# Factor blocks split into gates and the rest, with y outputs copied earlier and the maximum of h taken earlier, in a fused attention and two-MoE kernel

## The chip, the cores and the metric

The kernel runs on one core of a Trainium2 chip. Its engines each work through a queue of their own in order: TensorE (PE) multiplies matrices, VectorE (DVE), ScalarE (ACT) and GpSimd (POOL) do elementwise work, and SyncE (SP) issues most DMA transfers; ACT issues those of y. The metric is the device time of one execution in microseconds (us), less is better.

## The reference

Three stages follow one another over 4608 tokens, all in float32. Weights of the two MoE stages come as float64.

```python
# attention in chunks of 64 tokens, 8 heads of 64
scores = scale * np.matmul(q_c, k_c.transpose(0, 1, 2, 4, 3))
attn = softmax(scores);  x = attn @ v_c          # x: 4608 x 512
# first MoE
h = x @ w_in                                     # 4608 x 1024
e = np.exp(h - h.max(-1));  solu = h * e / e.sum(-1)
ln = (solu - mu) / np.sqrt(var + 1e-06) * g_ln
y = ln @ w_out                                   # 4608 x 512
# second MoE
g = y @ w_gate;  val = y @ w_val                 # 4608 x 1536
out = (g * sigmoid(g) * val) @ w_out2            # 4608 x 512
```

## The kernel before

Every product is made of three passes over a high part and a low part of each operand, so each weight and each result has to be split: ACT copies the high part, then DVE or POOL subtracts it from the value to leave the low part.

**Phase 1** makes y, 128 tokens at a time, in 36 slots, `slot(t)` for t = 0 to 35. From slot 3 on the engines' queues follow the order in which the code is written (`manual_schedule`). In one slot TensorE does, in order:

- `scores(t+2)`: s, for a tile of tokens two slots ahead
- `hidden(t)`: h, 24 matmuls
- `ln_T(t-1)`: tr, eight transposes of the slot before
- `pv(t+1)`: o, attention times v
- `y_run`: 32 of y's matmuls. An output y takes 24 of them, so it ends in the middle of a slot; the matmuls already done of the current output at the start of a slot are 0, 8 or 16, in turn. This number is called the slot's **y phase**: it is 0 in slots 10, 13, 16 and so on to 34, 8 in slots 11, 14, ..., and 16 in slots 12, 15, ...
- `p_transpose(t+2)`: pt, four transposes of the softmax. pt shares two PSUM buffers (tag `y`) with the outputs y, and takes the one of the output that ended first in this slot, so it needs the copy of that output (ACT, `ysb`, L162).

Around these, DVE takes the maximum and the difference of s (mx, e), converts one weight (L103, L109, L114, L120), sums the softmax (su, r), takes the maximum of h (nm, L341), finishes the layer norm's first half (se to nmu, so), and makes low parts (lnT, x). ACT does exp of e, exp of h (eh), copies lnT and x, squares (eh, L369, called the Square below), takes the sign off the next weights (L87), copies ysb and pbd. POOL adds the halves of a converted weight (L130, L133), scales e (L284; pt needs it) and finishes the layer norm (L371 to L383).

From slot 8 on each slot also converts one or two pieces of the second MoE's weights, 36 in all: for each of twelve factors f a **gate** piece g, a **value** piece v and an **out** piece o. `w2_out` gives g and v their places in one tile `blk` of eight parts (tag `blk`, one buffer): two for the gate (a11, a12), two for the value (a21, a22) and four for sums (s1 to s4), the operands of a Strassen-like product with seven products instead of eight. In the slot after the value's, three steps follow (`w2_spill`): `sums` makes s1 to s4 on DVE (L208), `high` copies seven parts on ACT into `shi` (L211) and stores them, `low` subtracts on DVE (L215) and stores them; both stores go to `ws_dram`. That slot is called a **spill slot** here. The pieces of seven slots, after which the pattern comes again with the next three factors:

| slot | 10 | 11 | 12 | 13 | 14 | 15 | 16 |
| --- | --- | --- | --- | --- | --- | --- | --- |
| converted | o0 | g1, v1 | o1 | g2 | v2, o2 | g3 | v3 |
| sums, high, low of | f = 0 | | f = 1 | | | f = 2 | |

So 17 is like 10, 18 like 11 and so on; the spill slots from 10 to 33 are 10, 12, 15, 17, 19, 22, 24, 26, 29, 31 and 33. The first piece of a slot is added on POOL ahead of the scaling of e, a second one at the slot's end.

In slots 0 to 5 the same three steps serve the first MoE's w_out (`split_scaled`): step 0 scales on ACT (L137), step 1 splits into wB on ACT and POOL (L71, L73), which `y_run` multiplies by from slot 5 on.

**Phase 2** reads y and the factors back and does the second MoE in six groups of tokens, `step(s, f)` for twelve f each, seven products per step from tiles `wsa` (the first four parts) and `wsb` (the other three).

Of the kernel before, what the change touches and what calls it, by code (L numbers as in the profile page):

```python
# [8 lines left out]
F32 = mybir.dt.float32  # L9
F32R = mybir.dt.float32r  # L10
# [3 lines left out]
AF = mybir.ActivationFunctionType  # L14
ALU = mybir.AluOpType
AX = mybir.AxisListType

P = 128
# [8 lines left out]
def attn_moe_moe2_kernel(  # L27
# [13 lines left out]
    nc = tc.nc  # L41
# [103 lines left out]
    NY = 3 * KF  # L145
# [22 lines left out]
    KH = KD // 2 * P  # L168
    NS = 7
    ws_dram = [dram.tile([P, NS, 2, KH], F32, tag=f"ws{f}", name=f"ws{f}") for f in range(FT)]  # L170
# [3 lines left out]
        f, j = divmod(u, 3)  # L174
        return raw_load(stage, (w_gate, w_val, w_out2)[j][f])

    blks = {}

    def w2_out(u):

        f, j = divmod(u, 3)
        if j == 2:
            return None
        if f not in blks:
            blks[f] = stage.tile([P, NS + 1, KH], F32, tag="blk", name="blk", bufs=1)
        return blks[f][:, 1:6:4] if j == 0 else blks[f][:, 0:8:7]

    def w2_spill(u, w):

        f, j = divmod(u, 3)  # L190
        if j == 0:
            return None
        if j == 2:
            hi = stage.tile([P, DM], F32R, tag="m", name="wohi", bufs=4)
            src, dst = w, wo_dram[f]
        else:
            b = blks.pop(f)
            hi = stage.tile([P, NS, KH], F32R, tag="shi", name="shi", bufs=1)
            src, dst = b[:, 1:], ws_dram[f].rearrange("p s b n -> p b s n")

        def sums():
            if j == 1:
                a21, a11, s1, s2, s3, a12, s4, a22 = (b[:, i] for i in range(NS + 1))
                for o, x, y, op in (
                    (s1, a21, a22, ALU.add), (s3, a11, a21, ALU.subtract),
                    (s2, s1, a11, ALU.subtract), (s4, a12, s2, ALU.subtract),
                ):
                    nc.vector.tensor_tensor(out=o, in0=x, in1=y, op=op)  # L208

        def high():  # L210
            nc.scalar.activation(out=hi, in_=src, func=AF.Copy)  # L211
            nc.sync.dma_start(out=dst[:, 0], in_=hi.bitcast(F32))

        def low():
            nc.vector.tensor_tensor(  # L215
                out=src.bitcast(F32R), in0=src, in1=hi.bitcast(F32), op=ALU.subtract
            )
            nc.sync.dma_start(out=dst[:, 1], in_=src)

        return sums, high, low  # L220

    with ExitStack() as ph1:
# [97 lines left out]
        def hidden(t, halves=(0, 1)):  # L320
            x = xt[t]
            if 0 in halves:
                ht[t] = ps_h.tile([P, DF], F32, tag="h", name="h")
            h = ht[t]
            for n in halves:
                i = 0
                for k in range(KD):
                    for a, b in PASSES:
                        nc.tensor.matmul(  # L329
                            h[:, n * DM:(n + 1) * DM], lhsT=x[:, a, k, :],  # L330
                            rhs=wA[:, n * KD + k, b, :],
                            start=(i == 0), stop=(i == 3 * KD - 1),
                        )
                        i += 1
            if 1 in halves:
                del xt[t]

        def ln_max(t):
            h = ht[t]
            nm = sm.tile([P, 1], F32, tag="nm", name="nm")  # L340
            nc.vector.tensor_reduce(out=nm, in_=h, axis=AX.X, op=ALU.max, negate=True)  # L341
            st["nm", t] = nm

        def ln_exp(t):
            h, nm = ht[t], st.pop(("nm", t))
            e = hp_.tile([P, DF], F32, tag="eh", name="eh", bufs=1)
            se = sm.tile([P, 1], F32, tag="se", name="se")
            nc.scalar.activation(out=e, in_=h, func=AF.Exp, bias=nm, accum_out=se)  # L348
            st["e", t] = e, se
# [93 lines left out]
        def y_upto(t):  # L443

            return max(0, min((NG - 1) * KD * NY, (t - GT) * KD * NY // GT)) if t >= W_OUT else 0
# [65 lines left out]
        wB = wblock(lastp, "B", KF)  # L511
# [14 lines left out]
        def slot(t, todo2):  # L526


            todo, ahead = w_todo(t), t + 2 < NT
            cs = conv.pop(t)  # L530
            outs = [w2_out(u) if k == "2" else None for k, u in todo]
            if ahead:
                scores(t + 2)
                if t + 4 < NT:
                    load_qk(t + 4)
                softmax(t + 2)
            cs[:1] = [conv_c(c, o) for c, o in zip(conv_b(cs[:1]), outs)]
            if ahead:
                softmax_b(t + 2)
            if t > 0:  # L540
                hidden(t)
            for k, steps in todo2:
                steps[0]()
            ln_max(t)
            ln_exp(t)
            ln_low = ln_T(t - 1) if t >= 1 else None
            ln_b(t)
            x_low = None
            if t + 1 < NT:
                pv(t + 1)  # L550
                if t + 3 < NT:
                    load_v(t + 3)
                x_low = x_split(t + 1)
            if ln_low:
                ln_low()
            if x_low:
                x_low()
            ln_c(t)
            for k, steps in todo2:
                steps[1]()  # L560
            if t + 1 < NT:
                conv_start(t + 1)
            cs[1:] = [conv_c(c, o) for c, o in zip(conv_b(cs[1:]), outs[1:])]
            y_run(wB, y_upto(t - 1), y_upto(t), ps_y, att)
            for k, steps in todo2:
                steps[2]()
            if t + 2 < NT:
                raws[t + 2] = w_raw(t + 2)
                p_transpose(t + 2)
            todo2 = []  # L570
            for (k, u), w in zip(todo, cs):
                if k == "o":
                    a, b = split_scaled(wB[:, u], w, g_sb[:, u:u + 1])
                    todo2.append((k, (a, b, lambda: None)))
                elif steps := w2_spill(u, w):
                    todo2.append((k, steps))
            return todo2
# [14 lines left out]
    with ExitStack() as ph2:  # L592
# [22 lines left out]
        def w_load(s, f):  # L615
            if f >= FT:
                s, f = s + 1, f - FT
            if s >= NSG:
                return
            if s == 0:  # L620
                nc.sync.dma_start(out=wout(f).bitcast(F32), in_=wo_dram[f])
            a = cp.tile([P, 4, 2, KH], F32R, tag="wsa", name="wsa", bufs=3)
            b = cp.tile([P, 3, 2, KH], F32R, tag="wsb", name="wsb", bufs=3)
            nc.sync.dma_start(out=a.bitcast(F32), in_=ws_dram[f][:, 0:4])
            nc.sync.dma_start(out=b.bitcast(F32), in_=ws_dram[f][:, 4:7])
            ws[s, f] = [a[:, i] for i in range(4)] + [b[:, i] for i in range(3)]

        def y_load(s):
            for kk in range(2):
# [196 lines left out]
```

## Time and profile before

| | |
| --- | --- |
| Median of three runs | 1539.91 us (1539.21 to 1540.45) |
| The profiled execution: its own time | 1538.05 us |
| The profiled execution: its span | 1536.1 us |
| Busy share of the span | PE 91%, DVE 59%, ACT 36%, POOL 32% |
| Mean granted TensorE clock | 0.957 of full speed |

The span is what the trace covers; 1.95 us of the profiled execution lie around it. A timeline row has the start and the duration in us, the engine, the line, out<-in, the shapes, the count, and in brackets the idle time ahead and what ended it. A row of windows has the stretch and its length, the busy us (and count) of PE, PEld (weight loads), DVE, ACT and POOL, the granted clock as a share of full speed, the DMA share and GB/s.

Slots are told apart in the trace by the start of their score matmuls: slot 10 starts at 205.84 us, slot 34 at 653.15 (it has no scores, so there its first matmul of h counts), phase 2's first product at 707.24.

### The profile page before, as it was taken

The page shows a single profiled execution, that of the slowest core. Times are in us where ns is not written, and L with a number is a line of the kernel's source. Part 1 is how long each engine was busy: PE and PEld are TensorE (multiplying, and loading weights), DVE is VectorE, ACT ScalarE, POOL GpSimd, SP SyncE. Part 2 cuts the span into 40 slices and gives each one's busy share as a digit, 9 for nine tenths or more (in the row PEclk, how much of TensorE's full clock was granted, in tenths as well). Part 3 has the DMA queues.
Part 4 walks back from the last instruction along what each step waited for, and adds up shares of the span by engine and source line. Part 5 has one row for each costly group of instructions (what it writes and reads, how often), then busy time and mean ns, then how long its engine had stood idle before and what let it go on. Part 6 is the DMA issues. An engine that isn't in the chain of part 4 may idle for free.

```text
span 1536.1 us, 21457 instructions
## 1 busy us (share of the span) xinstructions
PE 1403.2 (91%) x7920; PEld 1268.5 (83%) x7920; DVE 903.4 (59%) x1620; ACT 560.2 (36%) x1116; POOL 484.4 (32%) x597
## 2 busy tenths in 40 slices
PE   3578998979869878899999999999999999999998
PEld 2457877858758767789998999899999989999997
DVE  8863577757656765755446444644644464455442
ACT  4443444524525443444223232322322242333221
POOL 5553334334333424433113122321411132232211
PEclk9788999979989998999999999999999999999999
DMA  7311345345544443349773556456455635554531
GB/s 243 115 41 45 110 137 178 105 153 153 168 125 153 155 144 114 109 159 401 249 253 132 203 176 215 154 174 221 148 185 192 232 126 202 176 205 165 173 136 42
DMA packets 122936, 252.02 MB, mean 164 GB/s; under 512 B 45520, under 2 KB 79312, under 8 KB 113616
## 3 DMA queue, kind: packets, MB, share of 16 engines
q1 hardware_dynamic: 115920, 241.21, 47.2%
q10 hardware_dynamic: 6912, 9.44, 1.7%
q8 instruction: 63, 1.03, 0.3%
q14 instruction: 41, 0.34, 0.1%
HBM read 203.43 MB, written 47.19 MB: 163 GB/s over the span
## 4 chain that ended last, share of the span: by engine, by line
PE 63%; DVE 7%; issue 3%; ACT 3%; DMA 2%; POOL 2%; SPq 0%; ACTq 0%; DVEq 0%; POOLq 0%
PE o L723 13%; PE pa L657 10%; PE pd L657 10%; PE pc L657 10%; PE tail L723 6%; PE h L329 5%; PE pb L657 5%; PE y L156 2%; DVE so L359 1%; PE s L260 1%; ACT eh L348 1%; DVE blk L208 1%; DVE nm L341 1%; ACT shi L211 1%; DMA ws<-blk 1%
## 5 line engine op out<-in xcount | busy, mean ns | idle before, releaser
L329 PE MATMUL h<-wA,x 128*128 128x512 f32 x864 | 229.4, 424 | 25.3 <-DVE wA L473 12.7
L329 PEld LDWEIGHTS h<-wA,x 128*128 128x128 f32 x864 | 173.5, 205 | 73.3 <-DVE wA L473 13.8
L156 PE MATMUL y<-lnT,wB 128*128 128x384 f32 x1152 | 212.3, 341 | 7.6 <-POOL wB L73 3.6
L156 PEld LDWEIGHTS y<-lnT,wB 128*128 128x128 f32 x1152 | 201.0, 190 | 14.1 <-issue 5.1
L714 POOL TENSOR_TENSOR uflow<-sa,uflow 128x384 fp32r<-128x384 f32 x72 | 73.5, 1021 | 414.0 <-ACT uflow L685 392.8
L714 DVE TENSOR_TENSOR uflow<-sb,uflow 128x128 fp32r<-128x128 f32 x72 | 28.2, 391 | 228.8 <-ACT uflow L712 228.8
L693 POOL TENSOR_TENSOR u<-u,p 128x384 f32<-128x384 f32 x72 | 73.0, 1014 | 192.2 <-DVE u L692 183.6
L723 PE MATMUL o<-wo,uflow 128*128 128x512 f32 x504 | 122.8, 392 | 0.0
L682 ACT ACTIVATE p<-pa 128x384 f32<-128x384 f32 x72 | 35.5, 492 | 233.1 <-PE pa L657 231.1
L348 ACT ACTIVATE eh<-h,nm 128x1024 f32<-128x1024 f32 x36 | 40.2, 1116 | 195.6 <-DVE nm L341 195.6
L723 PEld LDWEIGHTS o<-wo,uflow 128*128 128x128 f32 x504 | 94.0, 188 | 18.1
L292 PE MATMUL pt<-ident,e 128*128 128x128 f32 x144 | 28.1, 331 | 82.5 <-POOL e L284 51.3
L292 PEld LDWEIGHTS pt<-ident,e 128*128 128x128 f32 x144 | 20.5, 169 | 88.8 <-POOL e L284 53.4
L695 ACT ACTIVATE sa<-pa 128x384 f32<-128x384 f32 x72 | 35.4, 492 | 149.1 <-PE pa L657 149.1
L657 PE MATMUL pa<-yk,wsa 128*128 128x384 f32 x432 | 88.6, 340 | 0.8 <-DVE osb L740 0.8
L723 PE MATMUL o<-uflow 128*128 128x512 f32 x360 | 87.5, 391 | 0.0
L657 PE MATMUL pa<-yk,wsb 128*128 128x384 f32 x432 | 86.6, 334 | 0.2 <-ACT p L682 0.2
L657 PE MATMUL pc<-yk,wsb 128*128 128x384 f32 x432 | 86.5, 334 | 0.0
L657 PE MATMUL pd<-yk,wsa 128*128 128x384 f32 x432 | 86.5, 334 | 0.0
L657 PE MATMUL pc<-yk,wsa 128*128 128x384 f32 x432 | 86.4, 334 | 0.0
L657 PE MATMUL pb<-yk,wsa 128*128 128x384 f32 x432 | 86.4, 334 | 0.0
L657 PE MATMUL pd<-yk,wsb 128*128 128x384 f32 x432 | 86.4, 334 | 0.0
(109 smaller groups left out, 2785.2 us busy)
## 6 DMA issues: line engine op xcount, KB each, us to landing
wsa<-ws SPq DMA_DIRECT2D x72, 1024.0 KB, 5.0
wsb<-ws SPq DMA_DIRECT2D x72, 768.0 KB, 4.3
ws<-shi SPq DMA_DIRECT2D x12, 896.0 KB, 4.5
ws<-blk SPq DMA_DIRECT2D x12, 896.0 KB, 6.7
raw<-in_moe_w_out SPq DMA_DIRECT2D x20, 512.0 KB, 7.2
qt<-in_q SPq DMA_DIRECT2D x36, 256.0 KB, 3.3
kbd<-in_k SPq DMA_DIRECT2D x72, 128.0 KB, 3.6
vt<-in_v SPq DMA_DIRECT2D x36, 256.0 KB, 2.7
```

Source lines behind the costliest of these rows:

```text
L156: nc.tensor.matmul(ys[u], lhsT=wB[:, f, a, d * P:(d + 1) * P], rhs=lnT[m][:, b, f, :], start=(n == 0), stop=(n == NY - 1),)
L208: nc.vector.tensor_tensor(out=o, in0=x, in1=y, op=op)
L211: nc.scalar.activation(out=hi, in_=src, func=AF.Copy)
L292: nc.tensor.transpose(pt[:, 2 * n:2 * n + 2].rearrange("p h i -> p (h i)"), e[:, n], ident)
L329: nc.tensor.matmul(h[:, n * DM:(n + 1) * DM], lhsT=x[:, a, k, :], rhs=wA[:, n * KD + k, b, :], start=(i == 0), stop=(i == 3 * KD - 1),)
L348: nc.scalar.activation(out=e, in_=h, func=AF.Exp, bias=nm, accum_out=se)
L657: nc.tensor.matmul(ps, lhsT=w[:, a, kk * P:(kk + 1) * P], rhs=yk[:, i, b, kk], start=(first and n == 0), stop=(n == 5), skip_group_check=True,
L682: nc.scalar.activation(out=p1, in_=psA, func=AF.Copy)
L693: nc.gpsimd.tensor_tensor(out=u3, in0=u3, in1=p5, op=ALU.add)
L695: nc.scalar.activation(out=sa, in_=psA, func=AF.Sigmoid)
L714: sub = lambda eng, o, x, h: eng.tensor_tensor(out=o, in0=x, in1=h.bitcast(F32), op=ALU.subtract)
L723: nc.tensor.matmul(o, lhsT=u[:, a, i * P:(i + 1) * P], rhs=wout(f)[:, b], start=(j0 and j == 0), stop=(j1 and j == 2),)
```

## The change

- The gate piece gets a tile of its own, `ga` (two parts, two buffers). `blk` keeps six parts (value and sums, one buffer). `sums` reads from both. `high` becomes two copies and `low` two subtractions and two stores, one for each tile; the parts stand in another order in `ws_dram`, so phase 2 finds its fifth product's operand in `wsa` and its fourth's in `wsb`.
- `ln_max` and `ln_exp` of a slot are written ahead of step 0 (`sums`, or the scaling of w_out in slots 3 to 5) instead of behind it.
- `y_run` is written in two pieces. The first runs up to the end of the output that is under way, and its copy `ysb` stands ahead of step 1 (`high`) and of the next slot's L87; the second stands where all of it stood. Where the y phase is 0, `y2` equals `y0` and the first piece is empty.

```diff
@@ -174,16 +174,17 @@
         f, j = divmod(u, 3)
         return raw_load(stage, (w_gate, w_val, w_out2)[j][f])
 
-    blks = {}
+    gates, blks = {}, {}
 
     def w2_out(u):
 
         f, j = divmod(u, 3)
-        if j == 2:
-            return None
-        if f not in blks:
-            blks[f] = stage.tile([P, NS + 1, KH], F32, tag="blk", name="blk", bufs=1)
-        return blks[f][:, 1:6:4] if j == 0 else blks[f][:, 0:8:7]
+        if j == 0:
+            gates[f] = stage.tile([P, 2, KH], F32, tag="ga", name="ga", bufs=2)
+            return gates[f]
+        if j == 1:
+            blks[f] = stage.tile([P, 6, KH], F32, tag="blk", name="blk", bufs=1)
+            return blks[f][:, 0:6:5]
 
     def w2_spill(u, w):
 
@@ -192,15 +193,17 @@
             return None
         if j == 2:
             hi = stage.tile([P, DM], F32R, tag="m", name="wohi", bufs=4)
-            src, dst = w, wo_dram[f]
+            dst, parts = wo_dram[f], [(w, hi)]
         else:
-            b = blks.pop(f)
+            b, g = blks.pop(f), gates.pop(f)
             hi = stage.tile([P, NS, KH], F32R, tag="shi", name="shi", bufs=1)
-            src, dst = b[:, 1:], ws_dram[f].rearrange("p s b n -> p b s n")
+            dst = ws_dram[f].rearrange("p s b n -> p b s n")
+            parts = [(g, hi[:, 0:2]), (b[:, 1:], hi[:, 2:])]
 
         def sums():
             if j == 1:
-                a21, a11, s1, s2, s3, a12, s4, a22 = (b[:, i] for i in range(NS + 1))
+                a11, a12 = g[:, 0], g[:, 1]
+                a21, s1, s2, s3, s4, a22 = (b[:, i] for i in range(6))
                 for o, x, y, op in (
                     (s1, a21, a22, ALU.add), (s3, a11, a21, ALU.subtract),
                     (s2, s1, a11, ALU.subtract), (s4, a12, s2, ALU.subtract),
@@ -208,14 +211,20 @@
                     nc.vector.tensor_tensor(out=o, in0=x, in1=y, op=op)
 
         def high():
-            nc.scalar.activation(out=hi, in_=src, func=AF.Copy)
+            for x, h in parts:
+                nc.scalar.activation(out=h, in_=x, func=AF.Copy)
             nc.sync.dma_start(out=dst[:, 0], in_=hi.bitcast(F32))
 
         def low():
-            nc.vector.tensor_tensor(
-                out=src.bitcast(F32R), in0=src, in1=hi.bitcast(F32), op=ALU.subtract
-            )
-            nc.sync.dma_start(out=dst[:, 1], in_=src)
+            for x, h in parts:
+                nc.vector.tensor_tensor(
+                    out=x.bitcast(F32R), in0=x, in1=h.bitcast(F32), op=ALU.subtract
+                )
+            if j == 2:
+                nc.sync.dma_start(out=dst[:, 1], in_=w)
+            else:
+                nc.sync.dma_start(out=dst[:, 1, 0:2], in_=parts[0][0])
+                nc.sync.dma_start(out=dst[:, 1, 2:], in_=b[:, 1:])
 
         return sums, high, low
 
@@ -539,10 +548,10 @@
                 softmax_b(t + 2)
             if t > 0:
                 hidden(t)
+            ln_max(t)
+            ln_exp(t)
             for k, steps in todo2:
                 steps[0]()
-            ln_max(t)
-            ln_exp(t)
             ln_low = ln_T(t - 1) if t >= 1 else None
             ln_b(t)
             x_low = None
@@ -556,12 +565,15 @@
             if x_low:
                 x_low()
             ln_c(t)
+            y0, y1 = y_upto(t - 1), y_upto(t)
+            y2 = min(y1, -(-y0 // NY) * NY)
+            y_run(wB, y0, y2, ps_y, att)
             for k, steps in todo2:
                 steps[1]()
             if t + 1 < NT:
                 conv_start(t + 1)
             cs[1:] = [conv_c(c, o) for c, o in zip(conv_b(cs[1:]), outs[1:])]
-            y_run(wB, y_upto(t - 1), y_upto(t), ps_y, att)
+            y_run(wB, y2, y1, ps_y, att)
             for k, steps in todo2:
                 steps[2]()
             if t + 2 < NT:
@@ -623,7 +635,7 @@
             b = cp.tile([P, 3, 2, KH], F32R, tag="wsb", name="wsb", bufs=3)
             nc.sync.dma_start(out=a.bitcast(F32), in_=ws_dram[f][:, 0:4])
             nc.sync.dma_start(out=b.bitcast(F32), in_=ws_dram[f][:, 4:7])
-            ws[s, f] = [a[:, i] for i in range(4)] + [b[:, i] for i in range(3)]
+            ws[s, f] = [a[:, 0], a[:, 2], a[:, 3], b[:, 0], a[:, 1], b[:, 1], b[:, 2]]
 
         def y_load(s):
             for kk in range(2):
```

ACT in slot 12 (y phase 16), from the Square on. Before:

```order
L369 ACTIVATE eh,sq<-so,nmu 128x1024
L211 ACTIVATE shi<-blk 128x1792
L87 ACTIVATE m<-raw 128x512
L162 ACTIVATE ysb<-y 128x384
L163 DMA y_2_76<-ysb 128x384
L162 ACTIVATE ysb<-y 128x384
L163 DMA y_3_77<-ysb 128x384
```

and of the change:

```order
L378 ACTIVATE eh,sq<-so,nmu 128x1024
L162 ACTIVATE ysb<-y 128x384
L163 DMA y_2_76<-ysb 128x384
L215 ACTIVATE shi<-ga 128x512
L215 ACTIVATE shi<-blk 128x1280
L87 ACTIVATE m<-raw 128x512
L162 ACTIVATE ysb<-y 128x384
L163 DMA y_3_77<-ysb 128x384
```

The first of the two copies ysb went ahead of the copies shi and of L87, and the one copy shi became two.

DVE in a spill slot, from the softmax's last step r to the layer norm's first step se. Before:

```order
L283 RECIPROCAL r<-su 128x8
L208 TENSOR_TENSOR blk<-blk 128x256 x4
L341 TENSOR_REDUCE nm<-h 128x1
L354 TENSOR_SCALAR se<-se 128x1
L356 RECIPROCAL rh<-se 128x1
```

and of the change:

```order
L292 RECIPROCAL r<-su 128x8
L350 TENSOR_REDUCE nm<-h 128x1
L211 TENSOR_TENSOR blk<-blk 128x256
L211 TENSOR_TENSOR blk<-ga,blk 128x256
L211 TENSOR_TENSOR blk<-blk,ga 128x256
L211 TENSOR_TENSOR blk<-ga,blk 128x256
L363 TENSOR_SCALAR se<-se 128x1
L365 RECIPROCAL rh<-se 128x1
```

The maximum nm went ahead of the four sums, which now read ga and blk and stand between nm and se.

POOL, with buffer numbers, from the addition of g3 in slot 15 to the scaling of e in slot 16. Before:

```order
L133 TENSOR_TENSOR blk_2629<-m_2574,raw_2458 128x2x256
L284 TENSOR_TENSOR e_2645<-e_2645,r_2656 128x512
L371 TENSOR_SCALAR v_2731<-sq_2729 128x1
L375 TENSOR_TENSOR rs_2733<-v_2731,mhalf_65 128x1
L377 TENSOR_TENSOR t2_2735<-rs_2733 128x1
L378 TENSOR_TENSOR t2_2735<-t2_2735,v_2731 128x1
L379 TENSOR_SCALAR t2_2735<-t2_2735 128x1
L382 TENSOR_TENSOR rs_2733<-rs_2733,t2_2735 128x1
L383 TENSOR_SCALAR so_2708<-so_2708,nmu_2711,rs_2733 128x1024
L93 TENSOR_SCALAR m_2745<-m_2745 128x512
L133 TENSOR_TENSOR blk_2629<-m_2745,raw_2618 128x2x256
L284 TENSOR_TENSOR e_2815<-e_2815,r_2826 128x512
```

and of the change:

```order
L133 TENSOR_TENSOR ga_2638<-m_2602,raw_2466 128x512
L293 TENSOR_TENSOR e_2654<-e_2654,r_2665 128x512
L380 TENSOR_SCALAR v_2740<-sq_2738 128x1
L384 TENSOR_TENSOR rs_2742<-v_2740,mhalf_65 128x1
L386 TENSOR_TENSOR t2_2744<-rs_2742 128x1
L387 TENSOR_TENSOR t2_2744<-t2_2744,v_2740 128x1
L388 TENSOR_SCALAR t2_2744<-t2_2744 128x1
L391 TENSOR_TENSOR rs_2742<-rs_2742,t2_2744 128x1
L392 TENSOR_SCALAR so_2717<-so_2717,nmu_2720,rs_2742 128x1024
L93 TENSOR_SCALAR m_2766<-m_2766 128x512
L133 TENSOR_TENSOR blk_2812<-m_2766,raw_2627 128x2x256
L293 TENSOR_TENSOR e_2828<-e_2828,r_2839 128x512
```

The order is the same. Before, g3 went into the new buffer blk_2629 ahead of the layer norm's steps and v3 into the same buffer a slot later; now g3 goes into ga_2638, and it is v3 that takes a new buffer of blk.

## Rows read from the trace of the kernel before

**Rows 1.** The profile's page, busy time by engine

```profile
PE 1403.2 (91%) x7920; PEld 1268.5 (83%) x7920; DVE 903.4 (59%) x1620; ACT 560.2 (36%) x1116; POOL 484.4 (32%) x597
```

**Rows 2.** Windows: slots 14, 15, 20, and slots 10 to 33 together

```profile
275.98:290.76 14.78, 14.78 (x102) 13.06 (x101) 11.61 (x22) 6.67 (x12) 6.13 (x10) 1.00 0.49 153
290.76:319.60 28.84, 15.47 (x101) 13.28 (x100) 14.83 (x25) 9.25 (x15) 6.89 (x10) 0.79 0.46 142
391.10:408.68 17.58, 17.34 (x101) 14.80 (x100) 9.97 (x19) 7.74 (x14) 6.22 (x12) 0.85 0.73 233
205.84:653.15 447.31, 377.46 (x2401) 327.41 (x2401) 304.93 (x525) 190.66 (x325) 170.50 (x254) 0.91 0.46 141
```

**Rows 3.** Waits from 205 to 655: us in total, times, longest

```profile
PE pt L292 <- POOL e L284: 38.7, 3, 13.4
PE pt L292 <- ACT ysb L162: 30.4, 8, 4.4
```

**Rows 4.** Timeline of TensorE, slot 14, which waits for nothing

```profile
275.98 1.09 PE L260 MATMUL s<-kbd,qt 128*64 128x128 f32 x16
277.01 5.74 PE L329 MATMUL h<-wA,x 128*128 128x512 f32 x24
284.57 5.82 PE L156 MATMUL y<-lnT,wB 128*128 128x384 f32 x32
290.23 0.60 PE L292 MATMUL pt<-ident,e 128*128 128x128 f32 x4
```

**Rows 5.** Timeline, end of slot 15

```profile
308.85 0.56 SPq L218 DMA_DIRECT2D ws<-blk  x1
316.23 1.28 POOL L133 TENSOR_TENSOR blk<-m,raw 128x512 f32<-128x512 f32 x1 [21.43 <-issue]
317.46 1.04 POOL L284 TENSOR_TENSOR e<-e,r 128x512 f32<-128x512 f32 x1
318.56 1.11 PE L292 MATMUL pt<-ident,e 128*128 128x128 f32 x4 [13.37 <-POOL e L284]
```

**Rows 6.** Timeline of GpSimd, slot 11

```profile
230.82 1.29 POOL L133 TENSOR_TENSOR blk<-m,raw 128x512 f32<-128x512 f32 x1 [4.26 <-DMA ws<-blk]
```

**Rows 7.** Timeline, slot 10 (from 205.84): DVE, ACT and TensorE

```profile
206.98 0.69 DVE L269 TENSOR_REDUCE mx<-s 128x8 f32<-128x512 f32 x1 [2.96 <-PE s L260]
212.29 2.37 DVE L208 TENSOR_TENSOR blk<-blk 128x256 f32<-128x256 f32 x4
214.58 1.22 DVE L341 TENSOR_REDUCE nm<-h 128x1 f32<-128x1024 f32 x1
217.07 0.15 DVE L354 TENSOR_SCALAR se<-se 128x1 f32<-128x1 f32 x1 [1.27 <-ACT eh L348]
220.19 1.68 ACT L211 ACTIVATE shi<-blk 128x1792 fp32r<-128x1792 f32 x1
221.90 2.03 DVE L215 TENSOR_TENSOR blk<-blk,shi 128x1792 fp32r<-128x1792 f32 x1 [1.17 <-ACT shi L211]
222.88 0.47 ACT L162 ACTIVATE ysb<-y 128x384 f32<-128x384 f32 x1
223.50 0.63 PE L292 MATMUL pt<-ident,e 128*128 128x128 f32 x4 [3.20 <-ACT ysb L162]
```

**Rows 8.** Timeline, slot 15: the sums, and a high part of 512

```profile
298.02 1.50 DVE L208 TENSOR_TENSOR blk<-blk 128x256 f32<-128x256 f32 x4
306.63 0.61 ACT L211 ACTIVATE wohi<-m 128x512 fp32r<-128x512 f32 x1
```

**Rows 9.** Timeline of DVE, slot 12 (from 238.87)

```profile
240.01 0.69 DVE L269 TENSOR_REDUCE mx<-s 128x8 f32<-128x512 f32 x1
249.32 1.22 DVE L341 TENSOR_REDUCE nm<-h 128x1 f32<-128x1024 f32 x1
```

**Rows 10.** Timeline of TensorE, slot 5

```profile
136.50 1.08 PE L156 MATMUL y<-lnT,wB 128*128 128x384 f32 x3 [3.41 <-POOL wB L73]
```

**Rows 11.** The page's DMA issues, phase 2: count, size, us to landing

```profile
wsb<-ws SPq DMA_DIRECT2D x72, 768.0 KB, 4.3
```

## Prediction

> **What bounds the kernel now.** The page's busy times come first: TensorE works 91% of the span, the others far less [rows 1]. So time is to be had only where TensorE stands. Phase 2 has next to no such places; phase 1 has them from slot 10 on, and there I measured by slots. A slot in which TensorE waits for nothing lasts 14.78 us at full clock, and its successor starts right behind pt [rows 2, 4]; I take 14.80. The 24 slots 10 to 33 lasted 447.31 us [rows 2], so they stand 447.3 − 24 × 14.80 = **92.1 us** above that. The view of waits says where: pt waited three times for POOL's e, 38.7 us, and eight times for ACT's ysb, 30.4 us [rows 3]. The remaining 23 us are slower matmuls behind these waits: slot 20 follows one of 4.4 us, has TensorE busy 17.34 of its 17.58 us, and a granted clock of 0.85, a mixture of 1.2 and 2.4 GHz [rows 2].
>
> The reader should see two different causes. **POOL:** in slot 15, g3 needs blk, whose contents of f = 2 are stored only at the end of that same slot. The store was issued at 308.85, POOL could add at 316.23, e behind it in the queue followed at 317.46 and pt at 318.56, 13.37 us late [rows 5]. Slots 22 and 29 are alike. **ACT:** in slot 10 ysb stands behind the copy shi and two copies of L87, and ends its wait at 222.88, so that pt starts at 223.50 [rows 7], 17.66 us into the slot in place of 14.25 [rows 4].
>
> **Part 1, the gate's own tile.** Nothing of f = 2 is in the buffer that g3 now takes: the last to use it was f = 1, stored at the end of slot 12. So the three POOL waits, 38.7 us, go with the slow clock behind them. The wait moves to the value: v3, first in slot 16, needs blk, stored at the end of slot 15. Queued behind it on POOL are e and the layer norm's steps. I put the subtraction's end in slot 15 at about 17.9 us after the slot's start (worked out below), hence the store at 3 us into slot 16; the landing took 316.23 − 308.85 = 7.4 us [rows 5], so v3 is added at some 10.4 and e is ready at 10.4 + 1.28 + 1.04 = 12.7, 1.5 us before pt asks. That POOL may wait without harm is seen in slot 11, where it stood 4.26 us for such a store and pt did not wait [rows 3, 6]. Bounds: nothing, or, if the store lands 3 us later, 1.5 us in each of slots 16, 23, 30.
>
> **Part 2, nm ahead of the sums.** In slot 10 (start 205.84) DVE is through with the softmax at 212.29, 6.45 us in, makes sums for 2.3 us, takes nm at 8.74, waits 1.27 us for eh and starts se at 11.23 [rows 7]. With the change nm starts when h ends, (277.01 + 5.74) − 275.98 = 6.77 [rows 4], and the sums lie in eh's shadow: 6.8 + 1.25 + sums. The sums took 2.37 us beside POOL's scaling of e, 1.50 in slot 15 where POOL stood still [rows 7, 8]. Now e is scaled beside nm, so I take 1.50, and se starts at 9.6, **1.65 us sooner**; so do the Square and all behind it. Bounds: 0.8 us sooner with 2.37, 1.65 with 1.50.
>
> The Trainium skill says in GPSIMD Engine Reference, Key points, that POOL shares its SBUF interfaces with VectorE and that they contend when a DVE instruction has two SBUF inputs. By that rule the sums are slow wherever POOL works beside them; the two durations agree with it. With the slow value in the nine spill slots that keep an excess the gain below would be 62 in place of 69.7; that is the first rival.
>
> **Part 3, ysb ahead of high.** Where the y phase is 8 or 16, the output ends 16 or 8 matmuls into y, at most 3 us after 8.59 [rows 4], before the Square is done. Then ACT does ysb right behind the Square and pt follows 0.62 later (222.88 to 223.50). Where the phase is 0, no matmul is moved, and ysb stays behind high: among the spill slots these are 10, 19, 22 and 31.
>
> **Part 4, the splits.** A copy of 512 takes 0.61, of 1792 1.68 [rows 7, 8]; 1280 in proportion 1.25. Two copies in place of one cost 0.1 us if the second starts before the first ends, as copies here do, 0.2 otherwise; I take 0.1. The subtraction, 2.03 before, becomes two, of 0.7 and 1.45, and the first does not wait for the second copy: 0.1. One more store on SP, 0.56 [rows 5], has slack: what queues behind it, loads for two slots ahead, is not waited for in these slots [rows 3].
>
> **What each slot becomes.** With n the start of nm, shi stood 220.19 − 214.58 = 5.6 behind it in slot 10; now the sums stand between, so the Square is done at P = n + 2.8 + 3.1 (n + 2.5 + 3.1 without sums). Then, with 14.25 for pt if it waits for nothing:
>
> - Slots 17, 24 (like 10, phases 8, 16): P = 12.7, pt at 14.25. Excess 0.
> - Slots 10, 31 (phase 0): shi 1.67, L87 twice 1.1, ysb at 15.5, pt at 16.1. Excess 1.85 each.
> - Slots 12, 26, 33 (like 12, phases 16, 8): here DVE sets n. mx at 240.01 to nm at 249.32, less the sums, makes 7.0 [rows 7, 9], so n = 8.2, P = 14.1, pt at 14.7. Excess 0.5 each.
> - Slot 19 (phase 0): P = 14.5, shi and one L87, pt 17.55. Excess 3.3.
> - Slots 15, 29 (phases 16, 8): n = 7.85, P = 13.75, pt at 14.35. Excess 0.1 each.
> - Slot 22 (phase 0): the same, then shi, wohi, L87: excess 2.85.
>
> Sum of the eleven spill slots: 3.7 + 1.5 + 3.3 + 0.2 + 2.85 = 11.55.
>
> What is late next: in phases 8 and 16 ysb and its DMA issue (0.9) push high back, and DVE's subtraction ends at P + 4.1: 2 to 3.6 us into the next slot (17.9 in slot 15), where mx stands behind it on DVE; the score matmuls would allow mx at 1.14 [rows 7]. Slot 13 (phase 0, behind 12): mx at 3.05, n = 8.45, then wohi and L87 twice ahead of ysb: pt at 16.3, excess 2.05. Slot 16: 1.1. Slots 25, 27, 30: 0.45, 0.4, 0.85. Together 4.85. For late clamps on POOL (L93, behind the layer norm) I add 1.5. For the clock I take 1.5 behind the waits of slots 19 and 22 and 3 behind the others of about 2 us; bounds 0 and, with 2.8 us as in slot 20 behind each wait of 1.8 or more, 14.
>
> Excess after: 11.55 + 4.85 + 1.5 + 4.5 = 22.4. Gain in slots 10 to 33: 92.1 − 22.4 = **69.7**.
>
> **At the start** the change costs: in slots 3 to 5 the scaling of w_out now stands behind eh, where it delays the split into wB by up to two copies of 0.7. In slot 5 y waits for wB, 3.41 us for POOL's share [rows 10]. I take 1.4 us, bounds 0 and 3. Phase 2's order of products and their matmuls are the same, and its loads have slack (last rival).
>
> **Sum.** 1538.05 (the profiled execution) − 69.7 + 1.4 = 1469.75; the median of the runs was 1.86 above that execution, so **1471.5 us**.
>
> **Rivals.**
> - *DVE is later than I think.* The sums stay at 2.37 beside POOL: 0.85 us in the nine spill slots where excess remains, 7.7 us, and as much again where the subtraction is late: 1480 to 1492. For it: DVE is busy 14.8 us in slot 15 alone [rows 2]. Against it: its mean is 304.93 / 24 = 12.7 [rows 2]. Chance 0.18.
> - *TensorE takes all.* POOL and the subtraction cost less than I charge, the clock never falls: 92.1 less only the four phase-0 waits' remainder, some 6, gives 1538 − 86 + 2 = 1454, at best 1448. Against it: ysb behind shi in phase 0 is certain. Chance 0.12.
> - *Only POOL's wait goes.* If DVE's late subtraction brings back 3 us at pt in most slots, 38.7 and the clock behind, 5, less 9 for ACT's waits that come up in slots 15, 22, 29 (3 × 3): 1540 − 35 = 1505. Against it: ysb no longer stands behind what is late. Chance 0.05, of which 0.01 for so much lateness that nothing is gained.
> - *Slower: phase 2 waits for its weights.* The fourth product reads wsb, a product earlier than before, and wsa comes free one product later, after the fifth. If a load were not landed, every one of 72 steps would wait. Landing takes 4.3 us at the median [rows 11] and the tile is loaded two steps ahead; to outweigh 69 us each step would have to lose 1 us, that is a load would have to take longer than two steps. Chance 0.02.
>
> **Chances.** Forecast (1455 to 1480) 0.63, then 0.18, 0.12, 0.05, 0.02. About 0.2% (3 us) is what a measurement of this kernel can tell from no change. Faster by more than that: 0.97; within it 0.01; slower 0.02. The range that holds 8 in 10 reaches into the two nearest rivals: 1451 to 1490.
>
> **What would show it.** POOL's wait for ws<-blk in slots 15, 22, 29 gone and a shorter one in 16, 23, 30; pt's wait for e gone. pt's wait for ysb small in phases 8 and 16, and still there in slots 10, 19, 22, 31 at 1.8 to 3.3 us. nm at 6.8 in slots like 10, the sums behind it at 1.5, se at 9.6. mx late in slots 13, 16, 18. The forecast is wrong if the sums keep 2.37, if the store of blk lands after 12 us in slot 16, or if the clock falls behind waits of 2 us.

## The result, and the profile after

The changed kernel took 1469.74 us (median of four runs, 1467.15 to 1470.92) against 1539.56 us before (1538.46 to 1540.45): 0.9545 of the time, interval 0.9528 to 0.9561. The profiled execution took 1469.27 us, with a span of 1467.5 us. The forecast was 1471.5.

The page's busy times, which answer to [rows 1]:

```profile
PE 1385.4 (94%) x7920; PEld 1255.2 (86%) x7920; DVE 905.3 (62%) x1632; ACT 561.7 (38%) x1128; POOL 491.0 (33%) x597
```

DVE, ACT and POOL work about as long as before. TensorE's busy time fell by 17.8 us although it runs as many matmuls; 15.1 of these lie in slots 10 to 33 (377.46 [rows 2] to 362.34 below), where fewer matmuls now run at a lower clock behind long waits. The rest of the gain is idle time gone.

Windows of slots 10 to 33 together, and of slots 13, 14, 19 and 20 (columns as in [rows 2]):

```profile
206.68:584.19 377.51, 362.34 (x2402) 315.87 (x2401) 302.86 (x534) 189.99 (x333) 174.64 (x250) 0.99 0.55 167
253.10:270.16 17.06, 14.99 (x102) 12.98 (x101) 12.63 (x21) 10.18 (x18) 8.70 (x15) 1.00 0.86 266
270.16:286.52 16.36, 16.36 (x102) 14.27 (x101) 11.63 (x22) 6.80 (x12) 6.15 (x10) 0.90 0.48 140
347.08:365.58 18.50, 14.98 (x102) 13.00 (x101) 16.57 (x28) 9.61 (x17) 10.11 (x16) 1.00 0.44 128
365.58:381.94 16.36, 16.36 (x101) 14.20 (x100) 10.59 (x19) 7.62 (x14) 5.96 (x10) 0.90 0.79 243
```

The 24 slots last 377.51 us, against 447.31 [rows 2]: **69.8 us less, where 69.7 were forecast**. That leaves 377.5 − 24 × 14.80 = 22.3 us of excess, where 22.4 were forecast. Slots 13 and 19 wait; slots 14 and 20, right behind them, wait for nothing and still last 16.36 us, at a granted clock of 0.90.

The view of waits, 205 to 600 us (as [rows 3]; the fourth and the fifth row show POOL waiting for the store of blk):

```profile
PE pt L301 <- POOL rs L391: 7.8, 4, 2.5
PE pt L301 <- ACT ysb L162: 6.3, 6, 3.5
PE pt L301 <- POOL t L386: 0.8, 1, 0.8
POOL blk L133 <- DMA ws<-blk: 9.1, 2, 4.9
POOL blk L133 <- issue: 5.8, 1, 5.8
```

The wait of pt for POOL's e is gone. What is left at pt comes to 14.9 us in 11 waits, against the 69.1 of [rows 3]. The names of the releasers mislead here: in the slots that name rs or t, pt also starts 0.61 to 0.63 us after the copy ysb began, just as in those that name ysb, so all three rows are waits for ysb. The next timeline, of slot 10 (from 206.68), shows one of them:

```profile
213.53 1.23 DVE L350 TENSOR_REDUCE nm<-h 128x1 f32<-128x1024 f32 x1 [0.30 <-PE h L338]
216.13 0.15 DVE L363 TENSOR_SCALAR se<-se 128x1 f32<-128x1 f32 x1
219.23 0.62 ACT L215 ACTIVATE shi<-ga 128x512 fp32r<-128x512 f32 x1
219.75 1.26 ACT L215 ACTIVATE shi<-blk 128x1280 fp32r<-128x1280 f32 x1
222.03 0.47 ACT L162 ACTIVATE ysb<-y 128x384 f32<-128x384 f32 x1
222.64 0.63 PE L301 MATMUL pt<-ident,e 128*128 128x128 f32 x4 [1.50 <-POOL rs L391]
```

Read it beside [rows 7]. nm starts 6.85 us into the slot in place of 8.74, se at 9.45 in place of 11.23, and no longer waits for eh. The y phase is 0 here, so ysb still stands behind shi, and pt starts at 15.96.

Timeline of slot 16 (from 301.30), the slot in which the value v3 now needs blk:

```profile
302.76 3.04 POOL L392 TENSOR_SCALAR so<-so,nmu,rs 128x1024 f32<-128x1024 f32 x1
302.80 1.49 DVE L220 TENSOR_TENSOR blk<-blk,shi 128x1280 fp32r<-128x1280 f32 x1 [0.47 <-ACT shi L215]
304.81 0.68 DVE L278 TENSOR_REDUCE mx<-s 128x8 f32<-128x512 f32 x1
305.27 1.19 SPq L227 DMA_DIRECT2D ws<-blk  x1
312.28 1.31 POOL L133 TENSOR_TENSOR blk<-m,raw 128x512 f32<-128x512 f32 x1 [5.78 <-issue]
313.55 1.04 POOL L293 TENSOR_TENSOR e<-e,r 128x512 f32<-128x512 f32 x1
315.77 0.66 ACT L87 ACTIVATE m<-raw 128x512 f32<-128x512 f32 x1 [0.20 <-DMA raw<-in_moe_w_out]
316.95 0.63 PE L301 MATMUL pt<-ident,e 128*128 128x128 f32 x4 [1.24 <-ACT ysb L162]
```

The store of blk is issued 4.0 us into the slot and lands 6.9 us later. POOL waits 5.78 us and adds at 10.98; e is ready at 314.59 − 301.30 = 13.29 us into the slot, before pt could start at 14.25. So the wait moved to a place where it costs nothing. The slot's 1.24 us at pt come from ysb, for two reasons. mx is late: 3.51 us in, behind DVE's subtractions, where 1.14 is possible. And L87, which stands ahead of ysb on ACT, waits 0.20 us for the load of the next weight: its issue on SP comes behind five stores, at 307.93, 6.6 us into the slot.

Outside these slots little moved. Slot 6 starts at 147.46 (146.61 before), the time from slot 34 to phase 2's first product is 55.0 us (54.1), and phase 2 lasts 828.3 us (828.9). Together with the 69.8 these make the 68.6 us by which the span shrank.

### The profile page after: what moved, and what is told of

The parts are those of the page before. It is cut to its first block, busy times and chain, and to the rows that moved or that the text cites. A ratio compares the mean times of both kernels' runs of the same rounds, so it can differ in the third digit from the quotient of the medians.

```text
span 1467.5 us, 21518 instructions
## 1 busy us (share of the span) xinstructions
PE 1385.4 (94%) x7920; PEld 1255.2 (86%) x7920; DVE 905.3 (62%) x1632; ACT 561.7 (38%) x1128; POOL 491.0 (33%) x597
## 3 DMA queue, kind: packets, MB, share of 16 engines
q8 instruction: 63, 1.03, 0.3%
## 4 chain that ended last, share of the span: by engine, by line
PE 75%; DVE 10%; POOL 4%; DMA 4%; issue 3%; ACT 3%; SPq 1%; ACTq 0%; POOLq 0%; DVEq 0%
PE o L735 14%; PE pa L669 10%; PE pd L669 10%; PE pc L669 10%; PE h L338 8%; PE y L156 7%; PE tail L735 6%; PE pb L669 5%; PE s L269 2%; DVE so L368 2%; DVE nm L350 1%; DMA raw<-in_moe_w_out 1%; DMA kbd<-in_k 1%; ACT eh L357 1%; POOL so L392 1%
## 5 line engine op out<-in xcount | busy, mean ns | idle before, releaser
L338 PE MATMUL h<-wA,x 128*128 128x512 f32 x864 | 221.5, 413 | 26.3 <-DVE wA L482 12.4
L338 PEld LDWEIGHTS h<-wA,x 128*128 128x128 f32 x864 | 167.6, 198 | 71.4 <-DVE wA L482 13.6
L669 PE MATMUL pa<-yk,wsa 128*128 128x384 f32 x864 | 175.0, 337 | 0.8 <-DVE osb L752 0.8
L669 PE MATMUL pd<-yk,wsb 128*128 128x384 f32 x864 | 172.9, 334 | 0.0
L669 PEld LDWEIGHTS pa<-yk,wsa 128*128 128x128 f32 x864 | 153.2, 188 | 7.6 <-DVE osb L752 2.9
L669 PEld LDWEIGHTS pd<-yk,wsb 128*128 128x128 f32 x864 | 151.8, 188 | 0.0
L708 DVE TENSOR_TENSOR sa<-pa,sa 128x384 f32<-128x384 f32 x72 | 40.2, 558 | 71.5 <-ACT sa L707 71.5
L735 PEld LDWEIGHTS o<-uflow 128*128 128x128 f32 x360 | 67.2, 188 | 13.2
```

Source lines behind the costliest of these rows:

```text
L338: nc.tensor.matmul(h[:, n * DM:(n + 1) * DM], lhsT=x[:, a, k, :], rhs=wA[:, n * KD + k, b, :], start=(i == 0), stop=(i == 3 * KD - 1),)
L669: nc.tensor.matmul(ps, lhsT=w[:, a, kk * P:(kk + 1) * P], rhs=yk[:, i, b, kk], start=(first and n == 0), stop=(n == 5), skip_group_check=True,
L708: nc.vector.tensor_tensor(out=sa, in0=psA, in1=sa, op=ALU.mult)
L735: nc.tensor.matmul(o, lhsT=u[:, a, i * P:(i + 1) * P], rhs=wout(f)[:, b], start=(j0 and j == 0), stop=(j1 and j == 2),)
```

## The experiments

Times are medians; each set was timed beside the kernel before on the same chip, at 1538.87 us for the first four and 1538.10 for the others.

**All but the gate's own tile.** The other two parts on the old single `blk`, with one copy, one subtraction and one store of low parts, all as in the kernel before. Of the edit, the tiles:

```diff
-            gates[f] = stage.tile([P, 2, KH], F32, tag="ga", name="ga", bufs=2)
-            blks[f] = stage.tile([P, 6, KH], F32, tag="blk", name="blk", bufs=1)
+            blks[f] = stage.tile([P, NS + 1, KH], F32, tag="blk", name="blk", bufs=1)
...
```

> Parts 2 and 3 without part 1 (blk keeps all eight parts). Theory (each cause costs what its slots show): the stores of f = 2, 5, 8 hold up POOL in slots 15, 22, 29 again, pt waits there three times for e, 12 to 13 us each, and the matmuls behind run slower: 1500 to 1512 us. Rival (the waits for POOL were only the visible end of a late chain of DVE and ACT, which parts 2 and 3 shorten as well): the three waits shrink to a few us, 1475 to 1485 us.

Measured: 1499.48 us, 0.9745 of before (0.9731 to 0.976), so the gate's tile, with its splits, is worth some 29 us on top of the other two. (This is against 1470.5, the mean of the changed kernel's two medians, 1469.74 and 1471.23; the second is that of its repeat below. So too in what follows.) A row of its waits, and windows of slots 14, 15 and 20:

```profile
PE pt L292 <- POOL e L284: 35.9, 3, 12.4
```

```profile
269.43:284.23 14.80, 14.80 (x102) 13.06 (x101) 11.62 (x22) 6.80 (x12) 6.13 (x10) 1.00 0.50 155
284.23:311.89 27.66, 15.50 (x101) 13.28 (x101) 14.74 (x25) 9.27 (x15) 6.91 (x10) 0.83 0.47 148
376.15:390.93 14.78, 14.78 (x101) 13.06 (x101) 10.46 (x20) 7.55 (x14) 6.44 (x10) 1.00 0.90 268
```

POOL's three waits are back nearly whole (35.9 us of the 38.7 before). The time is half a microsecond below the range of the theory and far from the rival's, which is out: nm and ysb being earlier takes only 2.8 us off these waits. Slots 14 and 20 ran at full clock here, though the slots ahead of them waited 2.1 and 3.0 us.

**All but nm ahead of the sums.**

```diff
-            ln_max(t)
-            ln_exp(t)
             for k, steps in todo2:
                 steps[0]()
+            ln_max(t)
+            ln_exp(t)
```

> Parts 1 and 3 without part 2 (sums ahead of nm again). Theory: the sums lie beside POOL's scaling of e and take 2.37 us again instead of 1.6, the wait of 1.27 us for eh comes back behind them, se starts 1.6 us later in slots like 10, and each spill slot that had an excess gains as much or more: 1485 to 1495 us, less 0.9 us given back in slots 3 to 5. Rival (DVE's work is the same, so its order is worth nothing once ysb goes ahead): 1468 to 1474 us.

Measured: 1493.73 us, 0.9709 (0.9695 to 0.9724): this part is worth some 23 us, and the theory holds. Timeline of its slot 10 (from 205.76):

```profile
212.46 1.04 POOL L293 TENSOR_TENSOR e<-e,r 128x512 f32<-128x512 f32 x1 [0.44 <-DVE r L292]
212.49 1.29 DVE L211 TENSOR_TENSOR blk<-ga,blk 128x256 f32<-128x256 f32 x1
213.71 0.41 DVE L211 TENSOR_TENSOR blk<-blk,ga 128x256 f32<-128x256 f32 x1
```

The 2.37 us of [rows 7] are explained: of four sums of 0.4 us one lasts 1.29, the one that starts while POOL scales e, and it ends 0.28 us after POOL's instruction. In the kernel before, the longest of the same four takes 1.29 us too. The Trainium skill says in SBUF — State Buffer, SBUF: two separate sides, that the interfaces which GpSimd and a VectorE instruction with two SBUF inputs share are a lock held for a whole instruction, not a shared bandwidth. The row agrees: one instruction stands still, and the sums beside it keep their 0.4 us.

**All but ysb ahead of high.**

```diff
-            y0, y1 = y_upto(t - 1), y_upto(t)
-            y2 = min(y1, -(-y0 // NY) * NY)
-            y_run(wB, y0, y2, ps_y, att)
             for k, steps in todo2:
                 steps[1]()
...
-            y_run(wB, y2, y1, ps_y, att)
+            y_run(wB, y_upto(t - 1), y_upto(t), ps_y, att)
```

> Parts 1 and 2 without part 3 (ysb behind shi and L87 in every slot). Theory: spill slots of phases 8 and 16 wait as those of phase 0 do now, 1.5 to 3.5 us each in 12, 15, 17, 24, 26, 29, 33, less what the later high costs the next slot: 1483 to 1493 us. Rival (the order on ACT only moves the wait, since high and low then come sooner): 1468 to 1476 us.

Measured: 1477.04 us, 0.9599 (0.9585 to 0.9613). This part is worth about 7 us: less than the theory, just more than the rival. Windows of slots 10 to 33, of slot 12 and of slot 13, then a timeline of the end of slot 12 and the start of slot 13 (from 254.92):

```profile
205.89:591.93 386.04, 362.20 (x2402) 315.88 (x2401) 303.54 (x536) 191.68 (x336) 172.22 (x254) 0.99 0.54 163
237.21:254.92 17.71, 15.35 (x101) 13.21 (x101) 15.56 (x26) 8.84 (x15) 9.52 (x14) 0.98 0.37 115
254.92:271.32 16.40, 16.15 (x102) 13.96 (x101) 10.59 (x19) 7.74 (x14) 5.94 (x11) 0.92 0.85 261
```

```profile
252.94 1.49 DVE L220 TENSOR_TENSOR blk<-blk,shi 128x1280 fp32r<-128x1280 f32 x1 [0.47 <-ACT shi L215]
254.59 1.20 POOL L392 TENSOR_SCALAR so<-so,nmu,rs 128x1024 f32<-128x1024 f32 x1
```

The seven spill slots in phases 8 and 16 (12, 15, 17, 24, 26, 29, 33) are 15.4 us longer together than in the changed kernel, which alone would have put the time into the theory's range; the 24 slots together are only 386.04 − 377.51 = 8.5 us longer. So 6.9 us of this part's gain are given back in other slots. How much exactly differs between executions: with the repeat of the changed kernel (below) the seven slots are 14.2 us apart and 3.4 are given back, mainly since its slots 14, 20 and 23 ran at full clock. The rows show one way: ysb first makes the copies and subtractions of high and low later. Here the subtraction ends at 254.43, ahead of POOL's so, which takes 1.20 us, and slot 16 lasts 14.78. In the changed kernel the subtraction runs into so (3.04 us in slot 16, above), POOL's next clamp and DVE's mx are late, and slot 16 lasts 16.21.

**The gate's own tile alone**, with both edits above undone.

> Part 1 alone. Theory (waits hide behind waits): the three waits for POOL go, but in the same slots 15, 22, 29 ysb now stands behind shi, wohi and L87 and is 4 to 5 us late, and DVE's late subtraction is no longer covered: 1507 to 1518 us, so the three parts alone gain less than together. Rival (the waits are independent): the 38.7 us and the slow matmuls behind them go whole, 1494 to 1500 us.

Measured: 1514.51 us, 0.9836 (0.982 to 0.9853). Its waits at pt from 205 to 600 us (slot 33 and its wait lie behind):

```profile
PE pt L301 <- POOL rs L391: 28.1, 10, 4.7
PE pt L301 <- ACT ysb L162: 13.5, 3, 4.5
```

As the theory had it, the waits for ysb that POOL's had covered come up in slots 15, 22 and 29, at 4.7 us each, and every spill slot waits 3.3 to 4.7 us. From the four kernels: on top of the tile alone nm first is worth 37.5 us (1514.51 − 1477.04) and ysb first 20.8 (1514.51 − 1493.73), the two together 44.0 (1514.51 − 1470.5), not 58.3. Both shorten the same wait.

**The changed kernel again**, with no edit.

> The changed kernel itself, on the chip of the next three, for differences below one per cent: 1467 to 1471 us.

Measured: 1471.23 us, 0.9561 (0.9548 to 0.9575), 0.2 us above what was expected. Windows of its slots 10 to 33 and of slots 13 and 14, which answer to the first three rows of the changed kernel's windows, then a row of ACT in slot 16 (from 300.16):

```profile
207.12:582.42 375.30, 359.19 (x2401) 313.54 (x2401) 301.80 (x534) 189.93 (x333) 174.52 (x250) 1.00 0.55 168
253.52:270.58 17.06, 14.99 (x101) 12.98 (x100) 12.63 (x21) 10.17 (x18) 8.70 (x15) 1.00 0.87 266
270.58:285.36 14.78, 14.78 (x101) 13.06 (x100) 11.61 (x22) 6.79 (x12) 6.14 (x10) 1.00 0.52 155
```

```profile
315.67 0.66 ACT L87 ACTIVATE m<-raw 128x512 f32<-128x512 f32 x1 [1.25 <-POOL t L386]
```

Slot 13 repeats to the hundredth; slot 14 does not: 14.78 us at full clock in place of 16.36 at 0.90. In this execution slot 17 is the one at 0.91, behind a wait of 2.26 us in slot 16. So whether the clock falls behind a wait of 2 us is not settled by the wait: it fell in three places in the one execution (4.4 us) and mainly in one in the other. The wait in slot 16 grew from 1.24 us because L87 waited 1.25 us there; the row names POOL, but the load of its weight was issued at 306.79 and took 8.8 us to land (7.8 in the first execution), and it is behind this that L87 starts.

**ysb ahead of high in phase 0 too.** There the output that ends 24 matmuls into y is also finished first:

```diff
-            y2 = min(y1, -(-y0 // NY) * NY)
+            y2 = min(y1, (y0 // NY + 1) * NY) if y0 else 0
```

> The change, and where the y phase is 0 the first 24 of y's matmuls are written ahead of high too, so that ysb stands right behind the Square in every slot. Theory (what is left of the waits stands behind shi, wohi and L87 in phase 0): pt's waits in slots 10, 13, 19, 22 and 31, 11 us in the changed kernel's trace, fall below 0.6 each, and with them the slow matmuls of slots 14, 20 and 23: 1453 to 1459 us. Rival (as with part 3, about half is given back since high and low come later and DVE starts the next slot late): 1460 to 1465 us.

Measured: **1459.48 us**, 0.9486 (0.9473 to 0.9499), some 11 us faster than the changed kernel. Its window of slots 10 to 33 and its one row of waits at pt, then a timeline of slots 10 (from 204.96) and 19 (from 342.03):

```profile
204.96:573.10 368.14, 357.96 (x2402) 312.19 (x2401) 302.01 (x534) 189.87 (x333) 176.72 (x250) 1.00 0.56 171
```

```profile
PE pt L301 <- ACT ysb L162: 10.2, 14, 1.3
```

```profile
218.06 0.49 ACT L162 ACTIVATE ysb<-y 128x384 f32<-128x384 f32 x1 [0.46 <-PE y L156]
219.25 0.60 PE L301 MATMUL pt<-ident,e 128*128 128x128 f32 x4
...
346.36 1.52 DVE L103 TENSOR_SCALAR m<-m 128x512 int32<-128x512 int32 x1 [0.77 <-POOL m L93]
351.42 1.17 DVE L350 TENSOR_REDUCE nm<-h 128x1 f32<-128x1024 f32 x1
357.15 0.47 ACT L162 ACTIVATE ysb<-y 128x384 f32<-128x384 f32 x1
357.76 0.63 PE L301 MATMUL pt<-ident,e 128*128 128x128 f32 x4 [1.32 <-ACT ysb L162]
```

Slot 10 waits for nothing, no wait at pt is above 1.32 us, and no clock falls behind one. Still the time lies between the two ranges, half a microsecond outside either: a part is given back once more. Slots 12 and 26 now last 16.3 us (15.1 and 15.2 in the changed kernel), and slot 19 has 1.3 us left: ysb stands right behind the Square there, and it is DVE that is late, with nm 9.4 us into the slot. Its conversion L103 waited 0.77 us for POOL's clamp L93, and then took 1.52 us.

**The same with the old order at the start** (nm behind step 0 while w_out is scaled, t ≤ `W_OUT`):

```diff
-            ln_max(t)
-            ln_exp(t)
+            if t > W_OUT:
+                ln_max(t)
+                ln_exp(t)
             for k, steps in todo2:
                 steps[0]()
+            if t <= W_OUT:
+                ln_max(t)
+                ln_exp(t)
```

> The kernel before this one, with the old order of nm and eh in slots 0 to 5. Theory (the scaling of w_out behind eh cost the 0.85 us by which slot 6 starts later in the changed kernel): slot 6 starts 0.8 to 1.4 us sooner than in ysb_first_phase0, and the time falls by as much. Rival (the later start is only how transfers fell in that execution): slot 6 starts within 0.3 us of the same time, and so does the end.

Measured: 1459.24 us, 0.9485 (0.9472 to 0.9498): no difference that can be measured, as the rival had it. Slot 6 agrees with neither expectation: it starts at 146.58, 0.85 us later than in the kernel above. Its start tells nothing here: it lies at 147.46 in the changed kernel, 147.89 in its repeat and 145.73 in the kernel with ysb first in phase 0, whose code is the same up to there. By the timelines the stretch from the pt at 114 us to slot 6 is 33.1 and 33.0 us with nm first (the changed kernel, and this kernel's counterpart above) and 32.7 with the old order, here and before; but it is 34.4 in the repeat of the changed kernel. So 0.3 to 0.4 us is what these four executions suggest for nm first at the start, and it isn't shown.

**The same with the gate's high part made early** (its copy moved from behind ysb to between nm and eh, so that low could end sooner):

```diff
+        def early():
+            if j == 1:
+                x, h = parts[0]
+                nc.scalar.activation(out=h, in_=x, func=AF.Copy)
...
-            for x, h in parts:
+            for x, h in parts[(j == 1):]:
...
             ln_max(t)
+            for k, steps in todo2:
+                if len(steps) > 3:
+                    steps[3]()
             ln_exp(t)
```

> As ysb_first_phase0, and the copy of the gate's high part (128x512) is made between nm and eh, where ACT waits, instead of behind ysb. Theory (the next slot starts late on DVE since low waits for the copies on ACT): low ends 0.5 us sooner, mx of slots 13, 16 and the like too, and the waits of 0.3 to 0.8 us there shrink: 1.5 to 3 us below ysb_first_phase0. Rival (DVE's own work sets it): within 1 us.

Measured: 1459.79 us, 0.949 (0.9477 to 0.9503): no gain, as the rival had it, but not for the rival's reason alone. Timeline of slot 10's end (from 206.96; slot 11 starts at 221.78) and of slot 13 (from 252.91):

```profile
210.15 0.62 ACT L216 ACTIVATE shi<-ga 128x512 fp32r<-128x512 f32 x1
219.98 0.68 DVE L225 TENSOR_TENSOR ga<-ga,shi 128x512 fp32r<-128x512 f32 x1
222.26 1.51 DVE L225 TENSOR_TENSOR blk<-blk,shi 128x1280 fp32r<-128x1280 f32 x1 [1.61 <-ACT shi L220]
223.70 0.68 DVE L283 TENSOR_REDUCE mx<-s 128x8 f32<-128x512 f32 x1
...
253.91 1.49 DVE L225 TENSOR_TENSOR blk<-blk,shi 128x1280 fp32r<-128x1280 f32 x1 [1.03 <-ACT shi L220]
253.92 1.53 POOL L393 TENSOR_SCALAR t<-t 128x1 f32<-128x1 f32 x1
257.76 0.43 DVE L103 TENSOR_SCALAR m<-m 128x512 int32<-128x512 int32 x1 [1.03 <-POOL m L93]
```

The step works: mx comes 1.9 us into slot 11 instead of 2.9 (222.66 − 219.78 in the kernel without it), and 2.4 into slot 13 instead of 2.9. But slots 10 to 33 take 368.20 us against 368.14, and slots 12, 19 and 26 last 16.3 us as before. What DVE gains at mx it loses at L103, which stands between mx and nm and waits for POOL's clamp L93: in slot 13 for 1.03 us in place of 0.40. The clamp stands behind the layer norm's so on POOL, and so ends 4.1 us into slot 13 where it ended 4.0: in the kernel without this step POOL lost the time beside DVE's subtraction in so itself (2.52 us), here in the small step L393 ahead of it (1.53 us, where it took 0.64). In slots 12, 19 and 26 L103 waits 0.76 us for the clamp as well and then takes 1.52 in place of 0.43, 1.85 us together, more than the 1.3 us that pt waits there. So what is left hangs on POOL's late steps as well as on DVE's own work, and not on when high is copied; no run takes POOL's part away alone.

Two buffers for blk as well, which would take POOL's remaining wait away, weren't tried.

## Why the prediction was right, step by step

It held for the path: POOL's wait for blk, then the chain of nm, se, the Square, high and ysb to pt. All figures below are of the changed kernel's profiled execution.

| Step | forecast | measured |
| --- | --- | --- |
| slots 10 to 33, gain | 69.7 | 69.8 |
| excess in the eleven spill slots | 11.55 | 11.8 |
| of it slots 10, 19, 22, 31 (phase 0) | 1.85, 3.3, 2.85, 1.85 | 1.7, 3.7, 3.1, 1.9 |
| of it the other seven spill slots | 1.7 | 1.4 |
| excess in slots 13, 16, 25, 27, 30 | 4.85 | 5.9 |
| late clamps on POOL, measured as the excess of 11, 18, 21, 28, 32 | 1.5 | 0.3 |
| lower clock, measured in slots 14, 20, 23 | 4.5 | 4.4 |
| start of slot 6 later | 1.4 | 0.85 (1.28 in the repeat); the part of nm first not shown |
| after slot 34, up to phase 2 | 0 | 0.9 later |
| phase 2 | 0 | 0.6 shorter |

- **The gate's tile.** POOL's wait for e is gone, and blk's moved to v3, as forecast: v3 added at 10.98 us (10.4 forecast), e ready at 13.29 (12.7), and pt did not wait for it.
- **nm ahead of the sums.** nm at 6.85 (6.77), the four sums in 1.5 us, se at 9.45 (9.6). The rival in which the sums keep 2.37 us is out, and the experiment without this part shows where those 2.37 came from.
- **ysb ahead of high.** Each slot's excess came within 0.6 us of the forecast, the late subtraction included: mx 2.9 us into slot 13 (3.05 forecast) and 3.5 into slot 16 (2 to 3.6).
- **The splits.** The two copies took 0.62 and 1.26 us (0.61 and 1.25). That the one more store on SP has slack did not hold in slot 16: it took 1.02 us there (0.56 forecast), ahead of the store of blk, which was issued at 4.0 us in place of 3, and ahead of the load that L87 waited for, 0.20 us in this execution and 1.25 in the repeat. How much of that wait is the one store and how much the late subtraction isn't shown.
- **The clock** was a guess between 0 and 14, and its 4.5 were right partly by luck. They were shared out as 1.5 behind slots 19 and 22 and 3 behind the other waits of about 2 us; measured are 2.8 (slots 20 and 23) and 1.6 (slot 14, behind 13), and nothing behind 10 and 31. The repeat shows fewer slots at a lower clock behind the same waits. One sign of being wrong that the prediction names, a clock that falls behind waits of 2 us, came about in slot 14, behind the 2.07 us of slot 13; it had a price in the sum, so it did not move the time.
- **Mis-sized:** the late clamps and the five slots 13 to 30 together were well sized (6.35 forecast, 6.2 measured); one by one they are off by 1.2 and 1.1, but a late clamp also acts inside those five (L103 waits 0.31 us for it in slot 16), so the two can't be told apart by slots. The start was over-charged by about 0.5. The sum for the profiled execution was 1469.75, and 1469.27 was measured; the 1.86 us added for the median of the runs were 0.5. That terms off by 0.5 to 1.2 us add up to 0.3 us is luck: in the repeat the 24 slots alone lasted 2.2 us less. **Not foreseen:** at the end of phase 1, y waits 3.96 us for lnT where it waited 2.87, which covers the 0.9 us there; why it does isn't shown:

```profile
619.91 19.45 PE L156 MATMUL y<-lnT,wB 128*128 128x384 f32 x96 [3.96 <-DVE lnT L416]
```

The other rivals are out too: if only POOL's wait had gone, 1505 would be left, and the tile alone took 1514.5; phase 2 did not wait for its weights. The case in which TensorE takes all (1448 to 1454) isn't reached even with ysb first in phase 0, because DVE stays late in slots like 12, in part behind POOL's clamp.

## What to carry to other kernels

Where two waits lie on one path, take them slot by slot: what removing the longer one is worth is set by the wait that lies under it (24 us alone, 29 with the others in place), and two edits that shorten the same wait don't add up (44 us, not 58). In an engine's queue the copy that releases the bottleneck engine belongs ahead of the copies that only have to be done by the next slot, in every phase of the pattern; but price what is then late, since here 3 to 7 of the 14 to 15 us that one such step gained came back in other slots, in part as late work on two other engines. Where a late step can be moved without moving the time, look for the wait that took its place: here DVE's maximum came sooner, and the conversion behind it waited for POOL instead.

## What the runs showed of the hardware

- **One instruction of DVE or POOL can stand still for the other's.** A sum of 0.4 us took 1.29 beside POOL's scaling. The other way round, POOL's so, 1.20 us alone, took 3.04 beside DVE's subtractions of 1.49 and 0.68 us, which kept their length although so had started 0.04 us earlier by the profile. DVE's L103, 0.43 us in the changed kernel's slot 16, took 1.52 in slot 19 of the kernel with ysb first in phase 0, beside POOL's addition of blk (346.30, 1.30 us), and it too ended 0.28 us after POOL's instruction (347.88 and 347.60). POOL's L393, a step on 128x1 that took 0.64 us in the counterpart, took 1.53 beside DVE's subtraction of 1.49, which had started 0.01 us earlier. The Trainium skill, in SBUF — State Buffer, SBUF: two separate sides, adds that whichever of the two starts first holds the lock; the sum and L393 agree, so does not by these starts, and spans on POOL are rough.
- **The granted clock behind a short wait differs between executions of one kernel.** Behind the same wait of 2.07 us it was 0.90 in one and 1.00 in the next, 1.6 us for that slot. In one variant it was 1.00 behind waits of 2.1 and 3.0 us.
